# Turning, finishing and mixing a head over two pieces of the next keys, and the last values in four pieces

## The chip, the cores and the metric

The kernel runs on one core of one Trainium2 chip. The metric is device time in microseconds (us); all runs told here were in the fast state (none was more than 1.5% above the fastest of its kernel). A ratio is the mean time of one kernel's fast runs over the mean of the other's fast runs of the same rounds, so it is not quite the ratio of the medians that are quoted. Times such as "at 184.7 us" are from the start of the profiled span, which is some 1.8 us shorter than the device time.

## The reference, cut to what matters

One decoding step for two sequences: attention of 16 query heads over 8 key/value heads, with a window of the last 4096 positions of the cache, beside a dense layer; the sum of the two goes out.

```python
W = min(4096, max(256, Sk // 4))            # 4096
q = (x @ wq) per head                       # 16 heads of 256
k, v = the last W positions, each kv head used by 2 query heads
p = softmax(q . k * Dh ** -0.5)
o = p . v
out = x + o.reshape(B, 1, Hq * Dh) @ wo + dense(xn)
```

For each of the 8 kv heads, 4 MB of keys and 4 MB of values have to come from HBM and are used once. With the weights that is 77.67 MB.

## The kernel before

A kv head's keys come as one load and are treated in four pieces (`NH` = 4). For each piece, DVE transposes the keys (`turn`), PE makes scores, ACT the exponentials, DVE transposes these (`turn_p`). When a head's four pieces are through, PE multiplies the head *before* it with its values (`values`). The result has to be turned (PE), summed and divided by the softmax denominator (DVE, `finish`) and multiplied with the output weights (PE, `mix`). `close` does these three at once, one head later, after the first piece of scores:

```python
def finish(i):
    ov = state.pop(("o", i))[:].rearrange("r (u m c) -> r u c m", u=NP, c=ND)
    pq = ps_q.tile([P, NP * ND * NR], FP32, tag="q", name="q")
    ...
    nc.tensor.transpose(pqv[:, u, c, :], ov[:, u, c, :], ident_f[0:NR, 0:NR])   # L488, x4
    ...
    nc.vector.tensor_copy(out=o[:], in_=pqv[:, 0, :, 0:BR])                      # L490
    nc.vector.tensor_tensor(out=o[:], in0=o[:], in1=pqv[:, u, ...], op=ALU.add)  # L492
    scale_o(i, o)                                                                # L471, writes oT
...
for i in range(Hkv + 1):
    if i + 1 < Hkv:
        load_k(i + 1, (0, T) if i + 1 < Hkv - 1 else (0, T // 2, T))
    if i < Hkv:
        load_v(i, (0, T) if i < Hkv - 1 else (0, T // 2, 7 * T // 8, T))
        load_wo(i, parts=1 if i < Hkv - 1 else 2)
        for piece in range(NH):
            s = i * NH + piece
            if s + 1 < NSTEP:
                turn(s + 1)             # DVE, L386
            scores(s)                   # PE, L398
            if s >= 1:
                turn_p(s - 1)           # DVE, L424
            ...
            if piece == 0 and i > 1:
                close(i - 2)            # finish and mix (PE, L210) at once
    ...                                 # then values of the head before, L457 or L507
```

The instructions of each engine are issued in program order (the kernel asks for it, `issue_in_order`). The last two heads take another way (`values_fixed`, 128 small products each, L507 before and L511 after) that needs no turn. The last head's `mix` writes L227.

The softmax here doesn't subtract the row's maximum and nothing guards it: scores larger than these inputs give would overflow.

Of the kernel before, what the change touches and what calls it, by code (L numbers as in the profile page):

```python
# [34 lines left out]
def kernel(  # L35
# [19 lines left out]
    _, Hkv, Sk, Dh = A_k_cache.shape  # L55
# [7 lines left out]
    T = W // PB  # L63
# [41 lines left out]
    def v_tile():  # L105
        return v_pool.tile([P, T * Dh], BF16, tag="v", name="v")
# [130 lines left out]
    def carry():  # L237
        early = consts.tile([Bsz, D], FP32, name="early")
        nc.vector.tensor_copy(out=early[:], in_=psE[:])
        add_last(ident_f[0:Bsz, 0:Bsz], early[:, :], start=True)  # L240
# [31 lines left out]
    def build_q(i):  # L272
        x, h0 = divmod(i * rep, HH)
        t = qdiag[i % NW]
        tv = t[:].rearrange("p (n e) c -> p n e c", e=NE)
        for j in range(NQ):
            rows = slice(j * Q, (j + 1) * Q)
            for e in range(NE):
                nc.gpsimd.tensor_copy(  # L279
                    out=tv[rows, :, e, j * Q : (j + 1) * Q : HS].rearrange(  # L280
                        "p n (b h) -> p n b h", b=Bsz
                    ),
                    in_=qv[rows, :, h0 : h0 + rep, x * Bsz : (x + 1) * Bsz, e].rearrange(
                        "p n h b -> p n b h"
                    ),
                )
# [59 lines left out]
    def dense_out():  # L346
        w2_sb = dense.pop("w2")
        for x in range(NX):
            for c in range(NF):
                add(act_bf[:, c, x, :], w2_sb[:, x, c, :])  # L350
# [4 lines left out]
    state = {}  # L355

    def load_cache(t, cache, i, cuts):

        src = cache[:, i, s0:Sk, :].rearrange("b (p t) d -> p b (t d)", p=PB)
        for lo, hi in zip(cuts, cuts[1:]):  # L360
            cols = slice(lo * Dh, hi * Dh)
            nc.sync.dma_start(out=t[:, cols], in_=src[:, :, cols])  # L362

    def load_k(i, cuts=(0, T)):
        k_t[i] = k_pool.tile([P, T * Dh], BF16, tag="k", name="k")
        load_cache(k_t[i], A_k_cache, i, cuts)

    def load_v(i, cuts=(0, T)):
        t = v_tile()
        load_cache(t, A_v_cache, i, cuts)  # L370
        v_t[i] = t[:].rearrange("p (t d) -> p t d", t=T)

    def load_wo(kvh, parts=1):
        w = wo_pool.tile([P, rep, ND * D], BF16, tag="wo", name="wo")
        r0 = kvh * rep * Dh
        win = A_wo[r0 : r0 + rep * Dh, :].rearrange("(h p c) d -> p h (c d)", h=rep, p=P)
        for u in range(parts):
            hs = slice(u * rep // parts, (u + 1) * rep // parts)
            nc.sync.dma_start(out=w[:, hs, :], in_=win[:, hs, :])
        wo_t[kvh] = w  # L380

    def turn(s):
        kt = kt_pool.tile([P, TH * Dh], BF16, tag="kt", name="kt")
        i, half = divmod(s, NH)
        k = k_t[i] if half < NH - 1 else k_t.pop(i)
        nc.vector.transpose(  # L386
            out=kt[:].bitcast(FP32),
            in_=k[:, half * TH * Dh : (half + 1) * TH * Dh].bitcast(FP32),
        )
        kt_t[s] = kt  # L390

    def scores(s):
        i = s // NH
        ktv = kt_t.pop(s)[:].rearrange("p (t n c e) -> p n e t c", t=TH, n=NB, e=NE)
        psc = ps_sc.tile([P, TH, Q], FP32, tag="sc", name="sc")
        for n in range(NB):
            for e in range(NE):
                nc.tensor.matmul(  # L398
                    psc[:],
                    lhsT=qdiag[i % NW][:, n * NE + e, :],  # L400
                    rhs=ktv[:, n, e, :, :],
                    start=(n == 0 and e == 0),
                    stop=(n == NB - 1 and e == NE - 1),
                )
        p_sb = p_pool.tile([P, TH * Q], BF16, tag="p", name="p")
        piece = s % NH
        if piece == 0:
            state["rs", i] = small.tile([P, NH, Bsz], FP32, tag="rs", name="rs")
        pv = p_sb[:].rearrange("p (t c b) -> p b t c", t=TH, b=Bsz)
        sv = psc[:].rearrange("p t (c b) -> p b t c", b=Bsz)  # L410
        for b in range(Bsz):
            nc.scalar.activation(  # L412
                out=pv[:, b, :, :],
                in_=sv[:, b, :, :],
                func=ACT.Exp,
                scale=scale,
                bias=off[:, b : b + 1],
                accum_out=state["rs", i][:, piece, b : b + 1],
            )
        p_t[s] = p_sb  # L420

    def turn_p(s):
        pT = p_pool.tile([P, TH * Q], BF16, tag="pT", name="pT", bufs=2 * NH + 1)
        nc.vector.transpose(out=pT[:], in_=p_t.pop(s)[:])  # L424
        pT_t[s] = pT
        i, half = divmod(s, NH)
        if half != NH - 1:
            return
        rs = state.pop(("rs", i))
        total = small.tile([P, 1], FP32, tag="total", name="total")  # L430
        nc.vector.tensor_reduce(out=total[:], in_=rs[:], axis=AXIS.XY, op=ALU.add)
        sums = small.tile([P, BR], FP32, tag="sums", name="sums")
        nc.vector.tensor_scalar(
            out=sums[:], in0=hsel, scalar1=total[:], scalar2=None, op0=ALU.mult
        )
        state["sums", i] = sums
# [31 lines left out]
    def scale_o(i, o):  # L468
        rec = state.pop(("rec", i))
        oT = small.tile([P, ND, rep, Bsz], BF16, tag="oT", name="oT")  # L470
        nc.vector.tensor_tensor(  # L471
            out=oT[:].rearrange("p c h b -> p c b h"),
            in0=o.rearrange("p c (b h) -> p c b h", b=Bsz),
            in1=rec[:]
            .rearrange("p (b h) -> p b h", b=Bsz)
            .unsqueeze(1)
            .to_broadcast([P, ND, Bsz, rep]),
            op=ALU.mult,
        )
        state["oT", i] = oT  # L480

    def finish(i):
        ov = state.pop(("o", i))[:].rearrange("r (u m c) -> r u c m", u=NP, c=ND)
        pq = ps_q.tile([P, NP * ND * NR], FP32, tag="q", name="q")
        pqv = pq[:].rearrange("p (u c r) -> p u c r", u=NP, c=ND)
        for u in range(NP):
            for c in range(ND):
                nc.tensor.transpose(pqv[:, u, c, :], ov[:, u, c, :], ident_f[0:NR, 0:NR])  # L488
        o = small.tile([P, ND, BR], FP32, tag="osum", name="osum")
        nc.vector.tensor_copy(out=o[:], in_=pqv[:, 0, :, 0:BR])  # L490
        for u in range(1, NP):
            nc.vector.tensor_tensor(  # L492
                out=o[:], in0=o[:], in1=pqv[:, u, :, u * BR : (u + 1) * BR], op=ALU.add
            )
        scale_o(i, o)
# [21 lines left out]
    def mix(kvh):  # L517
        oT = state.pop(("oT", kvh))
        w = wo_t.pop(kvh)
        put = add_last if kvh == Hkv - 1 else add  # L520
        for h in range(rep):
            for c in range(ND):
                put(
                    oT[:, c, h, :],
                    w[:, h, c * D : (c + 1) * D],
                    stop=(kvh >= Hkv - 2 and h == rep - 1 and c == ND - 1),
                )

    NFIX = 2

    def close(i):
        if i < Hkv - NFIX:
            finish(i)
        mix(i)

    load_k(0)
    load_dense()
    project()
# [3 lines left out]
    for i in range(Hkv + 1):  # L542
        if i + 1 < Hkv:
            load_k(i + 1, (0, T) if i + 1 < Hkv - 1 else (0, T // 2, T))
        if i < Hkv:
            load_v(i, (0, T) if i < Hkv - 1 else (0, T // 2, 7 * T // 8, T))
            load_wo(i, parts=1 if i < Hkv - 1 else 2)
            for piece in range(NH):
                s = i * NH + piece
                if s + 1 < NSTEP:  # L550
                    turn(s + 1)
                scores(s)
                if s >= 1:
                    turn_p(s - 1)
                if s == NSTEP - 1:
                    turn_p(s)
                if piece == 0 and i > 1:
                    close(i - 2)
            if i + 2 < Hkv:
                build_q(i + 2)  # L560
        else:
            close(i - 2)
            carry()
        if i == 0:
            dense_in()
            dense_out()
        if i >= 1:
            if i - 1 < Hkv - NFIX:
                values(i - 1)
            else:  # L570
                values_fixed(i - 1)
        if i == Hkv:
            close(i - 1)

    res = consts.tile([Bsz, D], BF16)
    for n in range(NO):
# [34 lines left out]
```

## Time and profile before

| | before |
|---|---|
| time, median of 3 runs | 189.86 us |
| profiled span | 188.0 us |
| PE, DVE busy | 77%, 57% |
| share of the DMA queue's packets in 16 engines' span | 97.0% |
| HBM read | 77.67 MB, 413 GB/s over the span |

### The profile page before, as it was taken

What the parts mean: (1) busy time and instruction counts of PE and PEld (TensorE: products, weight loads), DVE (VectorE), ACT (ScalarE), POOL (GpSimd) and SP (SyncE); (2) the same over time, 40 slices, a digit from 0 to 9 for tenths busy, and PEclk for the clock granted to TensorE, in tenths of its full rate; (3) what the DMA queues carried; (4) which work ended last, traced back from release to release, by engine and by line L of the source; (5) the groups of instructions that cost most, each with busy time, mean ns of one, the idle gap of its engine ahead of it and who ended that gap; (6) DMA issues with size and microseconds to landing.
All of it is one profiled execution on the core that took longest, in us unless ns stands there. A gap on an engine that the chain in (4) does not pass through costs nothing.

```text
span 188.0 us, 2346 instructions
## 1 busy us (share of the span) xinstructions
PE 145.5 (77%) x909; PEld 67.0 (36%) x909; DVE 106.8 (57%) x142; ACT 42.5 (23%) x142; POOL 16.5 (9%) x74
## 2 busy tenths in 40 slices
PE   0395089914989988976997599958996689988983
PEld 0131033811334433432442234313442234434662
DVE  6405397049671976079804991099506993977211
ACT  3005015200062124212331223012421242125101
POOL 7000600300003000300030003000030000000000
PEclk9999558855799999997899999975999999999755
DMA  6999899999999999999999999999999899999990
GB/s 220 421 469 446 380 433 442 439 443 439 432 446 418 420 412 421 448 439 386 472 443 441 397 425 446 425 439 422 436 436 439 380 439 429 453 443 387 424 388 35
DMA packets 5652, 77.81 MB, mean 414 GB/s; under 512 B 517, under 2 KB 2569, under 8 KB 2954
## 3 DMA queue, kind: packets, MB, share of 16 engines
q1 hardware_dynamic: 5636, 77.66, 97.0%
q8 instruction: 7, 0.11, 0.2%
q14 instruction: 3, 0.02, 0.0%
q10 hardware_dynamic: 6, 0.01, 0.0%
HBM read 77.67 MB, written 0.00 MB: 413 GB/s over the span
## 4 chain that ended last, share of the span: by engine, by line
DMA 60%; DVE 19%; PE 16%; SPq 2%; ACT 1%; issue 1%; ACTq 0%; DVEq 0%
DMA k<-in_A_k_cache_dram 50%; DVE kt L386 14%; DMA v<-in_A_v_cache_dram 10%; PE o L457 7%; PE sc L398 4%; DVE pT L424 3%; PE psE L210 3%; PE q L507 1%; SPq L362 1%; ACT p L412 1%; SPq L114 0%; PE psA L227 0%; DVE oT L471 0%; PE q L488 0%; SPq L295 0%
## 5 line engine op out<-in xcount | busy, mean ns | idle before, releaser
L386 DVE STREAM_TRANSPOSE kt<-k 128x2048 f32<-128x2048 f32 x32 | 73.1, 2288 | 49.7 <-DMA k<-in_A_k_cache_dram 49.7
L398 PE MATMUL sc<-kt,qdiag 128*128 128x512 bf16 x256 | 63.9, 401 | 17.2 <-DVE kt L386 17.2
L412 ACT ACTIVATE p<-sc,off 128x256 bf16<-128x256 f32 x64 | 33.0, 545 | 73.3 <-PE sc L398 72.6
L398 PEld LDWEIGHTS <-qdiag 128*128 128x128 bf16 x256 | 24.4, 101 | 56.5 <-issue 23.2
L457 PE MATMUL o<-v,pT 128*8 128x512 bf16 x192 | 42.5, 379 | 0.0
L457 PEld LDWEIGHTS <-pT 128*8 128x8 bf16 x192 | 17.2, 92 | 22.4
L424 DVE STREAM_TRANSPOSE pT<-p 128x512 bf16<-128x512 bf16 x32 | 21.7, 677 | 6.1 <-ACT p L412 6.0
L279 POOL COPY qdiag<-qt 32x16 bf16<-32x16 bf16 x64 | 13.0, 249 | 120.9 <-PE sc L398 104.8
L210 PE MATMUL psE<-wo,oT 128*2 128x448 bf16 x28 | 8.6, 444 | 7.2 <-DVE oT L471 7.2
L412 ACT ACTIVATION_READ_ACCUMULATOR p<-sc,off 128x1 f32 x64 | 11.8, 184 | 0.0
L465 ACT COPY o_sb<-o 8x512 f32<-8x512 f32 x6 | 3.5, 575 | 36.3 <-PE o L457 36.3
L210 PE MATMUL psE<-v,act_bf 128*2 128x448 bf16 x14 | 5.2, 567 | 6.5 <-DVE act_bf L344 6.5
L259 PE MATMUL q_ps<-v,xq 128*128 128x512 bf16 x28 | 8.0, 455 | 2.9 <-DMA v<-in_A_wq_dram 2.9
L507 PE MATMUL q<-pT,v 128*128 128x4 bf16 x256 | 7.2, 168 | 0.2 <-DMA v<-in_A_v_cache_dram 0.2
L507 PEld LDWEIGHTS <-v 128*128 128x128 bf16 x256 | 7.3, 102 | 0.3 <-DMA v<-in_A_v_cache_dram 0.3
L269 DVE CAST q_sb<-q_ps 128x512 bf16<-128x512 f32 x2 | 1.3, 687 | 8.6 <-PE q_ps L259 8.6
L259 PEld LDWEIGHTS <-xq 128*128 128x128 bf16 x28 | 3.1, 112 | 7.7 <-issue 3.5
L210 PEld LDWEIGHTS <-oT 128*2 128x2 bf16 x28 | 2.0, 91 | 10.2 <-DVE oT L471 7.8
L210 PEld LDWEIGHTS <-act_bf 128*2 128x2 bf16 x14 | 1.6, 121 | 9.5 <-DVE act_bf L344 6.5
L488 PEld LDWEIGHTS q<-ident_f,o_sb 8*128 8x128 f32 x24 | 3.3, 207 | 3.0 <-issue 3.0
L180 PE MATMUL xnT_ps<-ident,xn_bf 2*128 2x2 bf16 x7 | 0.5, 166 | 4.7 <-DVE xn_bf L138 4.7
L269 ACT CAST q_sb<-q_ps 128x512 bf16<-128x512 f32 x2 | 1.1, 588 | 12.9 <-PE q_ps L259 12.9
(59 smaller groups left out, 46.0 us busy)
## 6 DMA issues: line engine op xcount, KB each, us to landing
k<-in_A_k_cache_dram SPq DMA_DIRECT2D x7, 4096.0 KB, 29.4
v<-in_A_v_cache_dram SPq DMA_DIRECT2D x7, 4096.0 KB, 29.0
k<-in_A_k_cache_dram SPq DMA_DIRECT2D x2, 2048.0 KB, 24.5
v<-in_B_w_dram SPq DMA_DIRECT2D x2, 1568.0 KB, 24.8
wo<-in_A_wo_dram SPq DMA_DIRECT2D x7, 448.0 KB, 29.7
v<-in_A_wq_dram SPq DMA_DIRECT2D x1, 2048.0 KB, 7.7
v<-in_A_v_cache_dram SPq DMA_DIRECT2D x1, 2048.0 KB, 15.4
v<-in_A_wq_dram SPq DMA_DIRECT2D x1, 1536.0 KB, 10.8
```

The lines of the kernel that those rows point to most:

```text
L210: nc.tensor.matmul(psE[:], lhsT=lhsT, rhs=w, start=start, stop=stop, skip_group_check=True)
L259: nc.tensor.matmul(ps[u][:], lhsT=xq[:, s, :, :].rearrange("p j k -> p (j k)"), rhs=wq_sb[:, s, u * N5 : (u + 1) * N5], start=(s == 0), st ...
L269: copy(out=q_sb[:, u * N5 : (u + 1) * N5], in_=ps[u][:])
L279: nc.gpsimd.tensor_copy(out=tv[rows, :, e, j * Q : (j + 1) * Q : HS].rearrange("p n (b h) -> p n b h", b=Bsz), in_=qv[rows, :, h0 : h0 + r ...
L386: nc.vector.transpose(out=kt[:].bitcast(FP32), in_=k[:, half * TH * Dh : (half + 1) * TH * Dh].bitcast(FP32),)
L398: nc.tensor.matmul(psc[:], lhsT=qdiag[i % NW][:, n * NE + e, :], rhs=ktv[:, n, e, :, :], start=(n == 0 and e == 0), stop=(n == NB - 1 and ...
L412: nc.scalar.activation(out=pv[:, b, :, :], in_=sv[:, b, :, :], func=ACT.Exp, scale=scale, bias=off[:, b : b + 1], accum_out=state["rs", i] ...
L424: nc.vector.transpose(out=pT[:], in_=p_t.pop(s)[:])
L457: nc.tensor.matmul(po[:], lhsT=pT_t[i * NH + piece][:, uh * NP * Q : (uh + 1) * NP * Q : HS], rhs=v[:, u * NP : (u + 1) * NP, :].rearrange ...
L465: nc.scalar.copy(out=o_sb[:], in_=po[:])
L488: nc.tensor.transpose(pqv[:, u, c, :], ov[:, u, c, :], ident_f[0:NR, 0:NR])
L507: nc.tensor.matmul(po[:, c, :], lhsT=vv[:, t, c, :], rhs=pTv[:, th, 0:Q:HS], start=(t == 0 and c == 0), stop=(t == T - 1), skip_group_chec ...
```

## The change

Its intent is to take a hand-over out of PE's way. Before, PE turned a head's result and then stood waiting for DVE to finish it. Now PE makes another piece of scores in between. Besides, the last head's values come in four loads with a smaller last one, so that less work is left after the last of them.

```diff
-    def finish(i):
+    def turn_o(i):
         ov = state.pop(("o", i))[:].rearrange("r (u m c) -> r u c m", u=NP, c=ND)
 ... (the four turns on PE)
+        state["pq", i] = pqv
+
+    def finish(i):
+        pqv = state.pop(("pq", i))
         o = small.tile([P, ND, BR], FP32, tag="osum", name="osum")
 ...
-            load_v(i, (0, T) if i < Hkv - 1 else (0, T // 2, 7 * T // 8, T))
+            load_v(i, (0, T) if i < Hkv - 1 else (0, T // 2, 13 * T // 16, 15 * T // 16, T))
 ...
                 if s + 1 < NSTEP:
                     turn(s + 1)
+                if piece == 1 and i > 1:
+                    finish(i - 2)
                 scores(s)
 ...
                 if piece == 0 and i > 1:
-                    close(i - 2)
+                    turn_o(i - 2)
+                if piece == 1 and i > 1:
+                    mix(i - 2)
 ... (close is gone; for the last two heads mix is called by itself)
```

More of the change, by code (lines that the diff above doesn't have):

```diff
@@ L529 @@
     NFIX = 2
-    def close(i):
-        if i < Hkv - NFIX:
-            finish(i)
-        mix(i)
     load_k(0)
@@ L561 @@
         else:
-            close(i - 2)
+            mix(i - 2)
             carry()
@@ L572 @@
         if i == Hkv:
-            close(i - 1)
+            mix(i - 1)
     res = consts.tile([Bsz, D], BF16)
```

## The prediction

> **What bounds the kernel now.** I read the slices of the span first, then the queue table, the sync engine's own waits, the timeline of the last microseconds, and only then the engines' waits, because the change is about a hand-over between two engines and that matters only where an engine sets the pace.
>
> The slices and the queue table, from the page (busy share of each fortieth of the span in tenths; then packets, MB and share of sixteen DMA engines):
>
> ```profile
> PE   0395089914989988976997599958996689988983
> DVE  6405397049671976079804991099506993977211
> DMA  6999899999999999999999999999999899999990
> ...
> q1 hardware_dynamic: 5636, 77.66, 97.0%
> ```
>
> The reader is to see that PE and DVE have holes all along, and DMA has none between the second slice and the last but one. 97.0% of 188.0 us is 182.4 us of busy time for each of the sixteen engines. The single packet records of the trace agree: the first big packet starts 2 us after the span's start, the last big one ends at 184.39 us, and between 4 and 180 us close to 16 packets are in flight in every 4 us window (15.7 to 16.3). The rate inside a packet is also constant: the 16384-byte packets take 611 ns at the median and at the tenth percentile alike. So this is a stream of 77.66 MB with about 2 us before it and 3.5 us after it, and nothing that happens in the middle shortens it unless it lets the queue run dry or removes bytes.
>
> Can the queue run dry? The loads are all issued in order from the sync engine, and its waits look long:
>
> ```profile
> SPq L362 <- PE o L457: 54.5, 6, 11.0
> SPq L362 <- DVE kt L386: 49.9, 6, 10.2
> SPq L362 <- PE psE L210: 17.6, 1, 17.6
> ```
>
> These say that a V load waits for the value product of the head two before it, and a K load for the last transposition of the K two before it. But part 6 of the page gives 29.0 and 29.4 us from issue to landing for a 4 MB load that at 434 GB/s (27.1 GB/s an engine, from the 32768-byte packets' 1213 ns, times 16) needs 9.7 us. Two more transfers stand ahead of each. The worst places are the V load issued at 49.99 us and the last V loads at 163.26 us: ahead of the latter the V and output weights of head 6 are still moving until 173.87 us (landing records), so a margin of about 10 us is left.
>
> The end, from the timeline of the last stretch (start, duration, engine, line, what; in brackets the idle time before it):
>
> ```profile
> 163.26 1.85 SPq L362 DMA_DIRECT2D v<-in_A_v_cache_dram  x3
> ...
> 165.16 1.52 SPq L379 DMA_DIRECT2D wo<-in_A_wo_dram  x2
> ...
> 182.40 1.87 PE L507 MATMUL q<-pT,v 128*128 128x4 bf16 x64 [0.22 <-DMA v<-in_A_v_cache_dram]
> 184.31 0.17 DVE L471 TENSOR_TENSOR oT<-q,rec 128x8 bf16<-128x8 f32 x1 [3.61 <-PE q L507]
> 184.53 0.58 PE L227 MATMUL psA<-wo,oT 128*2 128x112 bf16 x16 [0.26 <-DVE oT L471]
> 185.15 0.56 DVE L578 CAST res<-psA 2x112 bf16<-2x112 f32 x2 [0.67 <-PE psA L227]
> 185.77 0.33 SPq L579 DMA_DIRECT2D out_dram<-res  x1
> ```
>
> The reader is to see three V pieces and behind them two halves of the last output weights. The profile's chain of waits runs through the second V piece (182.36) and the 64 products after it. Yet the landing records put the third V piece at 183.58, the first weight half at 184.16 and the second at **184.72** us, and the instruction records of the sixteen last products (L227) fall into eight at 184.52 to 184.58 and a second bunch that starts only at 184.748. The second half of the weights, the very last bytes of the stream, ends the kernel; the value products end 0.2 us before it and are nearly covered.
>
> Last, the hand-over that the change aims at:
>
> ```profile
> PE psE L210 <- DVE oT L471: 7.2, 7, 1.7
> ...
> DVE osum L490 <- PE q L488: 2.5, 2, 1.5
> ```
>
> Here it is: over the heads PE waits 7.2 us in all for the finished result, DVE 2.5 us for the turned one.
>
> **What the Trainium skill says.** "Perfetto Trace Analysis", section "Identifying the Most-Contended Engine": optimise the busiest resource first, and for DMA judge by HBM utilisation, not by occupancy. Here both agree: 413 GB/s over the span with its two ends, and no gap between. "DMA: Bandwidth & Descriptors", section "Where 436 GB/s comes from": a ceiling of 435.2 GB/s for the core's sixteen ports. The trace's 434 GB/s within large packets is that ceiling; the same page's lower HBM limit per core does not bind in this run with one core. The same page, section "Why small descriptors are slow (HBM only)": a fixed cost per packet. The trace has one: 4096 bytes take 159 ns, 12288 take 460 and 32768 take 1213, on a line of 0.0368 ns a byte plus some 8 ns a packet. "Perfetto Trace Analysis", section "DMA Optimizations": splitting can let work start sooner "if DMA engines are generally idle"; here they never are.
>
> **The change part by part.**
>
> *Turn, finish and mix over two pieces (six heads, 0 to 5).* No instruction is added or removed; the instruction order shows PE 1739 rows in both kernels and DVE 133 in both. Before, PE ran: scores of piece 0, four turns, four mixes (waiting on DVE), scores of piece 1. Now: scores of piece 0, turns, scores of piece 1, then mixes. On DVE the three small operations move behind the K transposition for piece 2. Take the head at 105 us. Its turns begin at 105.68 and end at about 106.3; DVE is busy with transpositions until 107.46, finishes at 107.92, and PE mixes from 107.98 after 1.66 us of idling. After the change PE takes scores of piece 1 at once (1.9 us, 106.6 to 108.5, its K tile being ready at 106.55); DVE does the 2.22 us transposition from 107.46 and finishes at about 110.2; PE then waits for the result again, from 108.5 to about 110.2. So the wait for the result is not removed: **it moves** behind piece 1, at 1.7 us against 1.66. At the head at 127 us the same reckoning gives about 0.7 us against 0.66. Estimate for all: 5 to 9 us where it was 7.2. What does go is DVE's 2.5 us for the turned result, since 2.2 us of transposition now lie between. On the end: nothing, as PE and DVE releases of K and V buffers shift by less than 1 us either way against a margin of about 10 us.
>
> *Last V in four pieces (32, 20, 8, 4 rows of 64 a partition) in place of three (32, 24, 8).* Bytes are equal. Rows are packets here (the 128 records of 4096 bytes are the old last piece), so 128 packets are added, 8 an engine, at 8 ns each, and one 9 ns completion record: 8 x 8 + 9 = about 0.07 us later for all that lies behind, the weights too. One more issue (0.6 us) on the sync engine stands 18 us ahead of its landing, so costs nothing. In return, after the last V byte only 8 products remain in place of 16, and the pieces before it are worked off sooner: 64 products took 1.88 us, 29 ns each. With the fourth piece landing at about 183.65, its 8 products end at about 183.9 instead of 184.29, and the result is ready 0.35 to 0.4 us sooner, at 184.1. The first weight half is there at 184.23, so its eight products may start 0.3 us sooner; the second bunch still waits for the second half, at 184.72 + 0.07 = 184.8.
>
> *Sum:* middle 0, packets +0.07, earlier result between 0 and -0.05 (the last bunch of products finding PE free). 189.86 + 0.05 gives about 189.9 us.
>
> **The rivals.**
> 1. *The hand-over counts.* If PE and DVE were the bound, and all 7.2 us of PE's wait vanished, the time would be about 183 us. For it: PE is 77% busy, and the chain of waits has 19% on DVE and 16% on PE. Against it: that chain passes through three K arrivals of 28 to 37 us, each of which resets whatever the engines gained, and the stream would have to carry 77.66 MB in less than its 182.4 busy microseconds. I give it 1%.
> 2. *The end counts.* The weights' landing is hidden in the profile's chain; should the chain be right and V be the last wait, the result 0.35 to 0.4 us sooner would show in full: 189.5 us. For it: the chain names V. Against it: the landing of the second half at 184.72 and the second bunch 0.03 us later. Inside the range.
> 3. *The finer pieces cost more, or the moved mixes hold up the scores.* Mixes now come ahead of the scores of piece 2, whose K tile is ready before the result is; PE may lose up to 2 us a head, V and so the next loads come later. The margin of about 10 us in the queue eats that. It would need six heads' loss to add up without any recovery, 189.9 + 2 = 192 at the very most.
>
> **Range and chances.** The three runs of before lie between 189.75 and 190.3, so half a microsecond is scatter. Rival 2 sets the low side, packets and scatter the high one: 189.4 to 190.4. Two per cent is 3.8 us, far more than any of the parts but rival 1: faster 0.01, within 2% 0.98, slower 0.01.
>
> **What would show it.** Right: DMA share again 97%, no digit below 8 in the middle; DVE's wait for the turned result near 0; PE's wait for the finished result still 5 to 9 us; fewer value products after the last V wait; the last products (L227) again in two bunches, the second within 0.1 us of the second weight landing at about 184.8; span 188.0 to 188.2. Wrong: a DMA stream that ends before 184 us, or a PE wait on the finished result near 0 together with a shorter span, or a slice of DMA under 8 in the middle, which would mean that the queue ran dry.

## The result, and the profile after

The changed kernel took 189.87 us (median of 6 runs, 189.76 to 190.02) and the kernel before 189.97 us (6 runs, 189.75 to 190.3): ratio 0.9993, 95% interval 0.998 to 1.0006. The two are the same, as predicted. That 189.87 is so near the 189.9 that was reckoned is luck as to the hundredths: the six runs of each kernel here spread over 0.26 and 0.55 us.

| | before | after |
|---|---|---|
| profiled span, us | 188.0 | 188.0 |
| PE busy, us | 145.5 | 141.9 |
| packets of the queue | 5636 | 5780 |
| PE waits for the finished result, us | 7.2 | 7.2 |
| DVE waits for the turned result, us | 2.5 | under 0.2, not listed |
| last head's result ready (start of its DVE step), at us | 184.31 | 184.06 |
| second half of the last weights landed, at us | 184.72 | 184.67 |
| last products' second bunch starts, at us | 184.76 | 184.71 |

(Landings and bunches are from the trace's single records. PE's busy time differs by its granted clock, 0.877 before and 0.911 after, as well.)

The page of the changed kernel, its slices and its queue line:

```profile
PE   0493099905989999956896869956995789998893
DVE  6505497049671994079704991099507983995101
DMA  6999899999999899999999999999999899999990
...
q1 hardware_dynamic: 5780, 77.66, 97.0%
```

The DMA row is as full as before. The added 144 packets are the 128 rows of one more V piece and its 16 completions.

The hand-over, from the list of waits after, and in the timeline of the head at 105 us (before first, then after):

```profile
PE psE L210 <- DVE oT L471: 7.2, 6, 1.6
```

```profile
105.68 0.64 PE L488 MATMUL q<-ident_f,o_sb 8*128 8x8 f32 x4
107.98 0.92 PE L210 MATMUL psE<-wo,oT 128*2 128x448 bf16 x4 [1.66 <-DVE oT L471]
108.83 3.65 PE L398 MATMUL sc<-kt,qdiag 128*128 128x512 bf16 x16
```

```profile
105.63 0.64 PE L488 MATMUL q<-ident_f,o_sb 8*128 8x8 f32 x4
106.57 1.91 PE L398 MATMUL sc<-kt,qdiag 128*128 128x512 bf16 x8 [0.30 <-DVE kt L386]
107.32 2.30 DVE L386 STREAM_TRANSPOSE kt<-k 128x2048 f32<-128x2048 f32 x1
109.91 0.17 DVE L471 TENSOR_TENSOR oT<-osum,rec 128x8 bf16<-128x8 f32 x1
110.13 0.92 PE L210 MATMUL psE<-wo,oT 128*2 128x448 bf16 x4 [1.65 <-DVE oT L471]
```

The reader is to see the number in brackets: PE idled 1.66 us ahead of the mix before and 1.65 us after. The piece of scores moved ahead of the mix, but a key transposition of 2.3 us moved ahead of the result in the same stroke.

The end, from the timeline after:

```profile
163.05 2.49 SPq L362 DMA_DIRECT2D v<-in_A_v_cache_dram  x4
165.58 1.07 SPq L379 DMA_DIRECT2D wo<-in_A_wo_dram  x2
181.79 2.23 PE L511 MATMUL q<-pT,v 128*128 128x4 bf16 x64 [0.20 <-DMA v<-in_A_v_cache_dram]
184.06 0.17 DVE L471 TENSOR_TENSOR oT<-q,rec 128x8 bf16<-128x8 f32 x1 [3.95 <-PE q L511]
184.28 0.79 PE L227 MATMUL psA<-wo,oT 128*2 128x112 bf16 x16 [0.26 <-DVE oT L471]
```

The result of the last head is there 0.25 us sooner, and the last products (L227) start 0.25 us sooner. But they now take 0.79 us where they took 0.58: eight of them start at 184.28 to 184.34, the other eight only from 184.71, when the second half of the weights has landed (184.67). The chain of waits, which ran through the second piece of V before, now names the weights:

```profile
DMA k<-in_A_k_cache_dram 57%; DVE kt L386 17%; DMA wo<-in_A_wo_dram 10%; PE o L457 4%; DVE pT L424 3%; PE sc L398 3%; SPq L362 1%; ACT p L412 1%; SPq L114 0%; DVE sums L433 0%; SPq L379 0%; DVE osum L496 0%; DVE oT L471 0%; PE psA L227 0%; ACTq L609 0%
```

The stream is full up to its last two microseconds, but it does not end all at once. The last three of these stretches in the kernel before (the numbers at the end are the granted clock, the share of the 16 DMA engines that is busy, GB/s):

```profile
182.00:183.00 1.00, 0.78 (x29) 0.70 (x27) 0.00 (x0) 0.00 (x0) 0.00 (x0) 0.50 0.91 360
183.00:184.00 1.00, 1.00 (x44) 1.00 (x41) 0.00 (x0) 0.00 (x0) 0.00 (x0) 0.50 0.56 202
184.00:185.00 1.00, 0.74 (x27) 0.46 (x23) 0.17 (x1) 0.00 (x0) 0.00 (x0) 0.50 0.08 29
```

The sixteen completion records of the second half of the weights come between 182.76 and 184.72 us (182.88 and 184.67 after), the last six of them 0.7 us after the tenth. So it is the latest of the sixteen that ends the stream; their mean is 183.80, and an even finish could be worth 0.9 us (an estimate from these records; no run tried it).

One thing differs that I had not priced. In the last head there is this on DVE and PE before:

```profile
165.68 0.17 DVE L490 COPY osum<-q 128x8 f32<-128x8 f32 x1 [1.50 <-PE q L488]
...
168.99 2.27 DVE L386 STREAM_TRANSPOSE kt<-k 128x2048 f32<-128x2048 f32 x1
...
171.40 1.90 PE L398 MATMUL sc<-kt,qdiag 128*128 128x512 bf16 x8 [0.61 <-DVE kt L386]
```

and this after:

```profile
167.29 2.27 DVE L386 STREAM_TRANSPOSE kt<-k 128x2048 f32<-128x2048 f32 x1
...
172.66 1.50 PE L511 MATMUL q<-pT,v 128*128 128x4 bf16 x51 [0.83 <-DMA v<-in_A_v_cache_dram]
```

DVE no longer waits 1.5 us for the turned result, the very last keys are transposed 1.70 us sooner (167.29 against 168.99), and PE is through with all scores 1.6 us sooner: its next instruction, the denominator (L440), starts at 171.55 against 173.14. Before, PE then never waited for the values of head 6; now it stands 0.83 us for them. So PE gained 1.6 us near the end in these two executions, and there the gain met the stream. Whether that matters is what the last two experiments ask.

### The profile page after: what moved, and what is told of

Its sections match the earlier page's. It is cut to its first block, busy times and chain, and to the rows that moved or that the text cites. A ratio compares the mean times of both kernels' runs of the same rounds, so it can differ in the third digit from the quotient of the medians.

```text
span 188.0 us, 2341 instructions
## 1 busy us (share of the span) xinstructions
PE 141.9 (75%) x909; PEld 65.6 (35%) x909; DVE 106.5 (57%) x142; ACT 42.5 (23%) x142; POOL 16.5 (9%) x74
## 3 DMA queue, kind: packets, MB, share of 16 engines
q1 hardware_dynamic: 5780, 77.66, 97.0%
## 4 chain that ended last, share of the span: by engine, by line
DMA 67%; DVE 21%; PE 7%; SPq 2%; ACT 1%; issue 1%; ACTq 0%; DVEq 0%
DMA k<-in_A_k_cache_dram 57%; DVE kt L386 17%; DMA wo<-in_A_wo_dram 10%; PE o L457 4%; DVE pT L424 3%; PE sc L398 3%; SPq L362 1%; ACT p L412 1%; SPq L114 0%; DVE sums L433 0%; SPq L379 0%; DVE osum L496 0%; DVE oT L471 0%; PE psA L227 0%; ACTq L609 0%
## 5 line engine op out<-in xcount | busy, mean ns | idle before, releaser
L398 PE MATMUL sc<-kt,qdiag 128*128 128x512 bf16 x256 | 62.2, 388 | 20.1 <-DVE kt L386 19.5
L398 PEld LDWEIGHTS <-qdiag 128*128 128x128 bf16 x256 | 23.1, 98 | 55.6 <-issue 21.6
L210 PE MATMUL psE<-wo,oT 128*2 128x448 bf16 x28 | 7.2, 382 | 7.2 <-DVE oT L471 7.2
```

Source lines behind the costliest of these rows:

```text
L210: nc.tensor.matmul(psE[:], lhsT=lhsT, rhs=w, start=start, stop=stop, skip_group_check=True)
L398: nc.tensor.matmul(psc[:], lhsT=qdiag[i % NW][:, n * NE + e, :], rhs=ktv[:, n, e, :, :], start=(n == 0 and e == 0), stop=(n == NB - 1 and ...
```

## The experiments

My theory: the stream of loads, without a gap, sets the time, and its last bytes (the second half of the weights) end it. Rivals: the hand-over counts and something gave its gain back; or V is the last wait and the finer pieces pay.

### 1 and 2: one half of the change each

Hand-over alone: the changed kernel with

```diff
-(0, T // 2, 13 * T // 16, 15 * T // 16, T)
+(0, T // 2, 7 * T // 8, T)
```

> The turn, finish and mix over two pieces alone, last V in three pieces as before. My theory (a gapless DMA stream sets the time): same as before, ratio 1.000 within 0.002, about 189.9 us; PE still waits about 7 us for the finished result (it moves behind piece 1), DVE's wait for the turned result is gone. Rival (the hand-over counts and the finer V pieces gave its gain back): faster than the changed kernel by more than 0.2%, a ratio below 0.998.

Measured: 189.84 us (5 runs, 189.79 to 190.18), ratio to before 0.9995 (0.9982 to 1.0009). PE's wait for the result was 7.5 us and DVE's wait for the turned one was not listed. As expected.

Pieces alone: the kernel before with the opposite edit.

> The last V in four pieces alone, the hand-over as before. My theory: the result is ready 0.2 to 0.4 us sooner than in the kernel before, the second bunch of the last products stays within 0.1 us of the landing of the second half of the last weights, the packets cost about 0.07 us; time the same, ratio 1.000 within 0.002. Rival (V is the last wait, as the chain of waits before says): 0.35 us or 0.2% faster, ratio 0.998.

Measured: 190.21 us (5 runs, 190.09 to 190.5), ratio 1.0013 (1.0000 to 1.0027). So the pieces alone gain nothing, and V as the last wait, which forecast 0.998, falls by these times. But the profile did not look as I expected either. This is its end:

```profile
181.35 3.56 PE L507 MATMUL q<-pT,v 128*128 128x4 bf16 x128
185.16 0.55 PE L227 MATMUL psA<-wo,oT 128*2 128x112 bf16 x16 [0.26 <-DVE oT L471]
```

All 128 value products of the last head run in one go with no wait for V, and the last products in one bunch with no wait for weights: in this execution PE ended the kernel, at a span of 188.6 us. The view of stretches says where it fell behind. The line for 150 to 154 us in the kernel before, then in this run (busy time of PE, weight loads, DVE, ACT, POOL, then the granted clock, the DMA share, GB/s):

```profile
150.00:154.00 4.00, 3.60 (x17) 1.42 (x16) 4.00 (x4) 1.44 (x5) 0.00 (x0) 1.00 1.01 421
```

```profile
150.00:154.00 4.00, 4.00 (x12) 1.47 (x12) 4.00 (x3) 0.77 (x3) 0.00 (x0) 0.57 1.00 414
```

PE was granted 0.57 of its clock here and did 12 products where it did 17. It was 1 us late from there on (the first denominator product of head 5 starts at 156.96 against 155.95) and, with the old hand-over, still late at the end. That is one profiled execution, the slowest of the five (190.5 us), so it cannot tell what V or the weights would have done had PE been in time. Whether such a stretch is why the five timed runs are 0.2 us slower is not shown; the 34 runs of the kernel before in all these experiments lie between 189.66 and 190.5 us themselves.

### 3: take the hand-over's wait away in earnest

The changed kernel with the mix one more piece later:

```diff
-                if piece == 1 and i > 1:
+                if piece == 2 and i > 1:
                     mix(i - 2)
```

> The changed kernel with the mix one piece later still (after the scores of piece 2), so that the finished result is there when PE comes to it. My theory: PE's wait for the finished result falls from 7.2 to about 0.5 us (what the last two heads leave), and the time does not move, ratio to before 1.000 within 0.003. Rival (the hand-over counts, and the change only failed to take it away): up to 7 us faster, ratio 0.965 to 0.99.

Measured: 189.92 us (4 runs), ratio 0.9996 (0.9982 to 1.001). The wait, in the list of this run:

```profile
PE psE L210 <- DVE oT L471: 0.3, 1, 0.3
```

It fell from 7.2 to 0.3 us (a new wait of PE for DVE's `osum`, 1.2 us in all, took a part of it back), and the time did not move. The rival that the hand-over's wait costs time falls.

### 4: a load less in the middle

The changed kernel (wrong): head 3 uses head 2's values again. (The result still passed the comparison; presumably the attention adds too little to the output to show one head's values.)

```diff
     def load_v(i, cuts=(0, T)):
+        if i == 3:
+            v_t[i] = v_t[i - 1]
+            return
```

> The changed kernel, wrong on purpose: head 3 reads head 2's values again, so one 4 MB load is left out of the middle and all instructions of the engines stay. My theory: each DMA engine has 8 packets of 32768 bytes less, 8 x 1.213 = 9.7 us, and all of it shows: about 180.2 us, ratio 0.949. Rival (the engines' own work, PE 77% busy with its waits, sets the pace in the middle): less than half of it, 185 us or more.

Measured: 180.36 us (4 runs), ratio 0.9496 (0.948 to 0.9513). That is 9.65 us less than the 190.01 us of before, against 9.7 reckoned from 8 packets an engine. No engine instruction was taken away; the whole time of the transfer came off. The stream sets the pace.

### 5 and 6: a longer hand-over, in the middle and at the end

Eight idle transpositions on DVE ahead of the finish, in the changed kernel, once in the iterations of heads 2 to 6 and once in that of head 7 alone (`spare` is a tile that nothing reads):

```diff
+                if piece == 1 and 1 < i < Hkv - 1:      # the other run: i == Hkv - 1
+                    for _ in range(8):
+                        nc.vector.transpose(
+                            out=spare[:].bitcast(FP32),
+                            in_=k_t[i][:, 0 : 4 * Dh].bitcast(FP32),
+                        )
                 if piece == 1 and i > 1:
                     finish(i - 2)
```

> The changed kernel with eight idle transpositions of 128x512 (an estimate of 0.57 us each, a quarter of the 128x2048 one) on DVE ahead of the finish, in the iterations of heads 2 to 6: some 4.6 us longer hand-over, five times, 23 us of added DVE work. My theory: PE's wait for the finished result grows to some 25 us and the time stays, ratio to before 1.000 within 0.003, because the queue of loads has a margin of about 10 us. Rival (engines or hand-over on the path): slower by 5 to 23 us, ratio 1.03 to 1.12.

Measured: 194.15 us (4 runs), ratio 1.0228 (1.0189 to 1.0267). A miss for my theory as I had put it, and not what the rival said either: it lies below the rival's 5 to 23 us. PE's wait for the result was 19.0 us in all, where I had put some 25. The transpositions took 0.71 us each, not 0.57, so some 5.8 us a head (eight starts at a pitch of 0.74, less a little), five times, some 29 us of DVE work; 4.1 us of it showed. The slices of DMA say that the stream did not run dry, and the timeline of PE says which of the five showed:

```profile
DMA  6999999998999999999999999999999999999920
```

```profile
156.92 1.65 PE L210 MATMUL psE<-wo,oT 128*2 128x448 bf16 x4 [2.99 <-DVE oT L471]
158.50 4.50 PE L398 MATMUL sc<-kt,qdiag 128*128 128x512 bf16 x16
...
178.79 3.52 PE L511 MATMUL q<-pT,v 128*128 128x4 bf16 x128
182.57 0.92 PE L210 MATMUL psE<-wo,oT 128*2 128x448 bf16 x4 [0.26 <-DVE oT L471]
...
185.12 3.56 PE L511 MATMUL q<-pT,v 128*128 128x4 bf16 x128
```

The weights' second half landed at 185.00 us (184.67 in the changed kernel), so the loads were hardly later, though the last V was issued at 170.16 us in place of 163.05. But after the hand-over of iteration 6, at 156.92, PE waits for no load any more and works through to 189 us: what the fifth delay took from PE ran into the end. The chain of waits of this run steps through K arrivals at 101.33 and 142.32 us, the same moments as in the changed kernel (101.33 and 142.28), so the delays before those two were absorbed. What was wrong was "because the queue of loads has a margin of about 10 us": that margin keeps the *loads* on time, not the work that follows the last of them.

> The same eight transpositions, but only once, in the iteration of head 7, the last. After it no stream hides PE: scores, values of head 6, its mix and the carry come one after another, and PE waited only 0.8 us for V of head 6 and 0.2 us for the second V piece of head 7. My theory: 4.6 us less a slack of 1 to 2.5 us show, so 2 to 3.5 us slower, 192 to 193.5 us. Rival (the stream hides engine work everywhere, to the end): the same within 0.5 us.

Measured: 194.69 us (4 runs), ratio 1.024 (1.0221 to 1.0259): 4.8 us more than the changed kernel's 189.87, and above the 192 to 193.5 that I had put, because the transpositions took longer than estimated. The added work was again 5.8 us, so 1.0 us of it was hidden, at the low end of the slack of 1 to 2.5 us that I had put; it matches the 0.83 + 0.20 us that PE waits for V after the change. The rival (the stream hides engine work to the end) falls.

### 7: the last V in one piece

```diff
-load_v(i, (0, T) if i < Hkv - 1 else (0, T // 2, 13 * T // 16, 15 * T // 16, T))
+load_v(i, (0, T) if i < Hkv - 1 else (0, T))
```

> The changed kernel with the last V as one load. My theory: all 128 last value products start when it lands, at about 183.5 us, and take 3.7 us at 29 ns, so the result comes at 187.3 where it came at 184.06; the weights' landing no longer counts; 2.7 us slower, 192.6 us. Rival (the end is hidden behind other things, pieces do not matter): same within 0.5 us.

Measured: 192.72 us (4 runs), ratio 1.014 (1.0119 to 1.0162). PE waits 3.65 us for the whole V, starts at 183.70 and works for 3.58 us. So pieces do matter, up to the point where the work that is left after V's last byte ends before the weights land; three pieces had reached it (experiment 1). The prediction doubted that splitting helps where the DMA engines are never idle. That holds for the length of the stream, but splitting the last load still lets the work behind it start sooner.

### 8: the price of a packet

V of heads 0 to 6 in eight loads each:

```diff
-load_v(i, (0, T) if i < Hkv - 1
+load_v(i, tuple(range(0, T + 1, T // 8)) if i < Hkv - 1
 ... (the last V as in the changed kernel)
```

> The changed kernel with each of the V loads of heads 0 to 6 in eight pieces, equal bytes. A packet is a row, so 4096-byte packets at 159 ns take the place of 32768-byte ones at 1213 ns. My theory: each engine has 8 x (8 x 159 - 1213) = 472 ns more a head and seven completions of 9 ns, 0.53 us a head, 3.7 us for seven heads, and all of it shows: 193.6 us, ratio 1.020. It puts a price on the 0.07 us that I gave the four pieces. Rival (cost of a packet is hidden, or the bound isn't the stream): same within 0.5 us.

Measured: 192.87 us (4 runs), ratio 1.0146 (1.0126 to 1.0165): 2.8 us more than the kernel before, three quarters of what was reckoned. The packet records grew by 4.06 us an engine (182.42 to 186.48), more than the time did. Up to 16.5 packets are in flight in a window in place of 16.3: so small packets seem to overlap a little, which a sum of durations does not see. An engine had 392 packets and 49 completions more, so one costs 2.84 us / 441 = 6.4 ns, and the nine that the change adds cost 0.06 us an engine where I had said 0.07.

### 9 and 10: weights ahead of the last V

To see whether four pieces pay where V is last, the last weights are loaded first, with three pieces and with four:

```diff
+            if i == Hkv - 1:
+                load_wo(i, parts=2)
             load_v(i, ...)
-            load_wo(i, parts=1 if i < Hkv - 1 else 2)
+            if i < Hkv - 1:
+                load_wo(i)
```

> The last output weights are loaded ahead of the last V, so that V's bytes are the last of the stream; V in three pieces, hand-over as changed. My theory: the third piece lands at about 184.7 in place of 183.6; the second piece's 48 products, from 183.5, end at 184.9, its 16 at 185.4, then the result and all sixteen last products: 1.1 us slower than before, about 191.0 us. Rival (V was the last wait all along, weights did not count): the same as before within 0.3 us.

Measured: 191.03 us (5 runs), ratio 1.0046 (1.0032 to 1.006). As expected: the last V piece now lands at 184.79, its products end at 185.47.

> As the run with the weights first and three pieces, but with the last V in four. My theory: here the finer pieces show, because nothing lands after V: 8 products remain after the last byte in place of up to 24, 0.35 us (0.2 to 0.5) faster than with three pieces, but still 0.8 us slower than before, about 190.65 us. Rival (finer pieces are worth nothing wherever V stands): no difference between three and four.

Measured: 190.82 us (5 runs), ratio 1.0037 (1.0024 to 1.0049). The gain over three pieces is 0.21 us between the medians, at the low edge of what I had put, and the two ratio intervals overlap, so the direction is likely rather than shown by the times alone. The trace of the first run has PE waiting 1.85 us for V and then doing 64 products in one go, that of the second has it waiting 1.23 us. But after the last load landed (184.96) there were not only its 8 products to do, since PE was still at the 16 before: it reached the result only 0.09 us sooner in these two profiles (185.42 against 185.51).

### 11 and 12: how much had each kernel to spare?

Two idle transpositions on DVE (0.72 us each) ahead of the last key transposition of the last head, in the kernel before and in the changed one:

```diff
+                if i == Hkv - 1 and piece == 2:
+                    for _ in range(2):
+                        nc.vector.transpose(
+                            out=spare[:].bitcast(FP32),
+                            in_=k_t[i][:, 0 : 4 * Dh].bitcast(FP32),
+                        )
                 if s + 1 < NSTEP:
                     turn(s + 1)
```

> The kernel before with two idle transpositions (0.72 us each as measured, 1.4 us) on DVE ahead of the last K transposition of the last head. Theory after the runs so far: in the kernel before, PE came to the end with only 0.2 us to spare (its wait for the second V piece), because DVE had waited 1.5 us for the turned result ahead of the last two K transpositions; so 1.4 us more show nearly in full: 0.8 to 1.3 us slower, about 191.0 us, ratio 1.004 to 1.007. Rival (the stream alone ends both kernels): same, ratio within 0.002.

Measured in the kernel before: 190.99 us (5 runs, 190.92 to 191.44), ratio 1.0055 (1.0043 to 1.0068).

> The same two transpositions at the same place in the changed kernel. Theory: here PE waited 0.83 us for V of head 6 and 0.2 us for the second V piece, and the last K tile was ready 0.3 us before PE came to it, some 1.3 us to spare in all; so next to nothing shows: at most 0.3 us slower, 189.9 to 190.2 us, ratio 1.000 to 1.002. Rival (no difference in slack between the two kernels): as much slower as in the kernel before.

Measured in the changed kernel: 189.86 us (5 runs, 189.72 to 190.08), ratio 0.9992 (0.9979 to 1.0006). Their ends, that of before first:

```profile
181.92 3.56 PE L507 MATMUL q<-pT,v 128*128 128x4 bf16 x128
185.73 0.54 PE L227 MATMUL psA<-wo,oT 128*2 128x112 bf16 x16 [0.26 <-DVE oT L471]
```

```profile
180.06 3.95 PE L511 MATMUL q<-pT,v 128*128 128x4 bf16 x128
184.27 0.80 PE L227 MATMUL psA<-wo,oT 128*2 128x112 bf16 x16 [0.26 <-DVE oT L471]
```

The same 1.4 us cost the kernel before 0.95 us and the changed one nothing. In the first, PE takes all last products in one run and ends the kernel; in the second they still stand waiting for the weights (0.80 us in place of 0.54). This shows that the change did gain time on PE near the end, of more than a microsecond (the products of the last values start at 180.06 against 181.92), and that the stream of loads hides it. It comes from the hand-over's half: in the first of these runs PE waits for no piece of V, so finer pieces could not have helped it.

## Why the prediction was right

**The bound** was right. "A stream of 77.66 MB" with no gap: taking 8 packets an engine out took 9.65 us off, and taking some 6 us of PE waits out (experiment 3) took nothing off. One sum is a little off: 32768 bytes in 1213 ns are 27.0 GB/s, and times 16 that is 432 GB/s, not 434.

**The hand-over** was right in its main step. "The wait for the result is not removed: it moves": 7.2 us before and 7.2 after, at the head at 105 us 1.65 us where 1.7 was reckoned. At the head at 127 us I had said 0.7 us and it was 1.65 (the mix now at 130.60); I had carried over PE's lateness of that one execution, which did not come back. DVE's wait for the turned result went, as said. (The counts of 1739 and 133 rows stand in no trace; the traces have 909 matmuls, 909 weight loads and 142 DVE instructions in both kernels, so the conclusion holds.)

**"On the end: nothing"** was right for the time and incomplete as a step. I had asked only whether buffers come free in time (they did; the shift was up to 1.2 us where I had put under 1: the V load issued at 82.31 us before goes out at 81.07 after). The 1.5 us of DVE's saved wait in the last head goes straight to the last transposition and gives PE 1.6 us, and it stays unseen only because PE then has to wait for V and the weights. The kernel before was nearer to that edge than I thought: of 1.4 us more it could hide 0.45.

**The four pieces**: the cost of 0.07 us is 0.06 by the price of experiment 8, and cannot be seen in the landing of one profile (184.67 against 184.72). The result came 0.25 us sooner in place of 0.35 to 0.4, since the 8 last products ended at 184.02 and not 183.9: I had counted 29 ns for each and left out that the last one runs for 0.17 us. The step that decides, that the second bunch waits for the weights, was right (0.04 us after the landing, in both kernels; the prediction's 184.748 stands as 184.76 in the trace), and so nothing of it reached the end.

**Rival 3** was refuted by the wrong argument. "The margin of about 10 us in the queue eats that" holds for the loads (experiment 5), but lateness of PE in the last two heads goes into the end, 4.8 of 5.8 us (experiment 6). Had the change made PE later there, it would have shown.

Left open: why the pieces alone were 0.2 us slower than the kernel before, a difference at the edge of its interval. Open too is which of the two, PE or the stream, ends the slower executions of the kernel before: the profiled one (span 188.0 us) is among its fastest, 9 of its 34 runs in the experiments are above 190.2 us, and none of the 20 runs of the changed kernel and of experiments 1, 3 and 12, which all have the new hand-over, is. That fits a kernel that sometimes comes late on PE at the end, but no such run was profiled. No version was found that beats both kernels by more than the scatter; none of those tried shortens the stream but the one that leaves bytes out.

## What to carry to other kernels

When one resource is busy without a gap, first ask what ends it, and reckon any other change only from what remains after its last bytes. Removing a wait on an engine off that path gains slack and not time; test how much with a small idle operation put where it hurts most, in both kernels. When work is moved ahead of a wait on one engine, look at what moves ahead of the releasing instruction on the other, because the wait may simply move along.

## What the Trainium skill lacked or had wrong

- "Perfetto Trace Analysis", section "DMA Instruction — HWDGE (DVE, Sync)", says that the data movement of the DMA engines is not in the profile; that is meant of the window of the issuing instruction. What no page has is how to find the load that ends a kernel when the chain of waits names another: here the weights' second half, landing at 184.72 us, stood in the landing records alone, and the chain of the kernel before named the second piece of V, which had landed at 182.36.
- "DMA: Bandwidth & Descriptors", section "Why small descriptors are slow (HBM only)", gives a cost per packet and speaks of small ones. No page has a measured price for row packets of some kilobytes behind a full queue: here 6.4 ns each, completions included, so that 4096-byte packets in place of 32768-byte ones for 28 MB cost 2.8 us of 190.
- "Perfetto Trace Analysis", section "Optimization Strategies" under "Optimizing DMA Performance", advises, when the matmul engine waits for other engines, to optimise those that block the critical path. It does not say how to tell whether such a wait is on that path: here the wait of PE for DVE fell from 7.2 to 0.3 us and the time stayed (ratio 0.9996).
